# A new issue order for the first batch of a bucketed attention with a gated projection, with unread matmuls and another PSUM home for scale scratch

## The chip, the core and the metric

The kernel runs on one core of a Trainium2 chip. The metric is the device time of one execution in microseconds (us). The engines are TensorE (PE in the profile), VectorE (DVE), ScalarE (ACT), GpSimd (POOL) and SyncE (SP), which here issues every DMA. Each engine works through its own instructions in the order in which they were issued to it. Where an instruction needs something of another engine or of a DMA, it waits on a semaphore, and everything behind it on its engine waits with it.

## The reference

Four batches of eight heads, 768 tokens and head size 64. Keys and queries get six sign bits from a projection; a query sees only keys with the same six bits. The attention output feeds two projections whose product is projected again.

```python
B, H, S, D = 4, 8, 768, 64
q_bucket = sum(((q @ proj) > 0) * 2 ** arange(6));  k_bucket = ...     # proj is 64 x 6
mask = q_bucket[:, :, :, None] == k_bucket[:, :, None, :]
scores = where(mask, (q @ k.T) / 8, -1e9)
attn = exp(scores - max(scores));  attn = attn / (sum(attn) + 1e-9)
x = (attn @ v).transpose(0, 2, 1, 3).reshape(3072, 512)
out = ((x @ w_a) * (x @ w_b)) @ w_out                                  # w_a, w_b: 512 x 1536
```

## The kernel before

Every float32 operand of a matmul is split into two 16-bit parts (a high one and the rest), scaled by powers of two, so one product takes two or three matmuls in 16 bits.

**Preparation.** Keys of two heads at a time (`kprep`), queries of all heads for a third of the sequence, called a chunk (`qprep`), and values (`vprep`) are loaded, their largest magnitude is found (L785, L782, L998), spread over all partitions by a small matmul against an identity (`spread`, L450), turned into a power of two (`scale_of`, L456 to L478), and the data are split (L922 ACT, L934 or L938 copy, L943 DVE). A transposition by DMA (L883) brings each half to the layout that PE wants; for the first key pair and the first query chunk PE transposes instead (L894, `turn`). Bucket bits come from a matmul of 12 columns (L855, `buckets`) and are written as marks (L868) beside the data, so that a score of unequal buckets comes out hugely negative. The weights are prepared in the same manner (`words`, `to_f32`, `w_scale`, `hi_lo`: L563 loads, L659 largest magnitude, L592, L599 and L606 joining, L678 or L679 and L683 splitting).

**Attention.** A unit is a batch, a chunk and half of the heads, written 0_0_1 for batch 0, chunk 0, half 1; it has eight tiles (`qtile`) of 128 queries by 768 keys, written 0_0_1_j_h_t. A tile goes scores on PE (L1065), largest on DVE (L1077), width and bias (L1086, L1093 or L1099), exponential on ACT (L1109), cast to 16 bits (L1117 to L1119), subtraction of the cast (L1129 on POOL or L1133 on DVE), DMA transposition (L1139), and attention times values on PE (L1148). Scores have two PSUM buffers (tag `s`). When a unit's tiles are done, `su_end` scales the result, and after the second half it makes `xT` for the chunk.

**Projections.** `moe` takes the 1536 inner columns in twelve blocks of 128. A block is 24 matmuls into a PSUM buffer `ab` (L1351), ACT (L1365), DVE (L1373), a cast (L1381 or L1385), POOL (L1393), then six matmuls into `o` (L1403). `ab` and `o` have one PSUM buffer each. Block 0_2_3 is batch 0, chunk 2, block 3.

**The order.** The functions only record operations. `ORDER` (L96 to L290) is a list of operation numbers in the order of issue; a number plus 10000 or 20000 picks another engine for an operation that has such a choice, and a negative number -n would call `fill(n)` (L1513), which issues n matmuls into a buffer called `warm` that nobody reads. The list before has no negative number. Each engine's order of work is the order of its operations in the list. A tile of PSUM or SBUF with one buffer is handed on in the same order, so a matmul into `o` waits until whoever had `o` before has been read.

Of the kernel before, what the change touches and what calls it, by code (L numbers as in the profile page):

```python
# [45 lines left out]
SUMS = [1, 0]  # L46
# [15 lines left out]
QK = float(2.0**14)  # L62
LEAST = 16.0
# [6 lines left out]
def constants():  # L70
# [219 lines left out]
]  # L290


# [1263 lines left out]
```

## Time and profile before

| what | us |
|---|---|
| median of 3 runs (lowest, highest) | 929.32 (927.99, 933.16) |
| the profiled execution, its own time | 935.07 |
| its span, first to last instruction | 933.0 |
| PE busy in the span | 848.7 |
| DVE, ACT, POOL busy in the span | 665.3, 542.3, 445.2 |

The profiled execution took 2.07 us more than its span, and 5.75 us more than the median of the runs. The page divides the span into 40 slices of 23 us. In its row for PE the first ten slices are below the rest, which stand at 9 (90% or more) nearly to the end; the row for DVE is high over the first twelve slices or so; and the row PEclk, the clock that was granted to PE in tenths of full speed, dips in slices 3 to 5.

### The profile page before, as it was taken

To read this page: it belongs to the slowest core of one execution; us is meant where nothing else is said; L and a number is where in the kernel's file an instruction comes from. 1 tells how busy PE (TensorE), PEld (TensorE's weight loads), DVE (VectorE), ACT (ScalarE), POOL (GpSimd) and SP (SyncE) were. 2 spreads that over 40 slices of the span, in tenths; PEclk is the share of its full clock that TensorE was granted. 3 is DMA by queue.
4 is the path that set the end of the run, shared out by engine and by line. 5 is a ranking of instruction groups with operands and counts; after the bars stand their busy time and mean duration, and the time that the engine had idled before them with its cause. 6 is when DMAs were issued, how large, how long until landed. Compare 5 with 4: busy or idle time off the path is not lost.

```text
span 933.0 us, 22762 instructions
## 1 busy us (share of the span) xinstructions
PE 848.7 (91%) x9042; PEld 632.3 (68%) x9042; DVE 665.3 (71%) x1576; ACT 542.3 (58%) x1039; POOL 445.2 (48%) x384
## 2 busy tenths in 40 slices
PE   2656696989999999999999999999999999999998
PEld 2334464666777777777777777777777777777775
DVE  7888889879887868877866756876877964752311
ACT  5887889778853566554545446553566646453222
POOL 1556857666753445453253264554444745352111
PEclk9956799899999999999999999999999999999999
DMA  8999999999598769989857657888968974744000
GB/s 321 215 236 227 219 214 235 234 195 232 132 183 176 133 133 203 194 170 198 161 90 139 129 124 173 155 160 178 188 157 166 165 124 93 142 109 69 1 24 22
DMA packets 445353, 149.69 MB, mean 160 GB/s; under 512 B 416960, under 2 KB 437568, under 8 KB 445248
## 3 DMA queue, kind: packets, MB, share of 16 engines
q1 hardware_dynamic: 445248, 148.25, 77.7%
q8 instruction: 70, 1.15, 0.5%
q14 instruction: 35, 0.29, 0.1%
HBM read 37.85 MB, written 6.29 MB: 47 GB/s over the span
## 4 chain that ended last, share of the span: by engine, by line
PE 50%; DVE 17%; DMA 8%; issue 5%; ACT 5%; POOL 3%; SPq 1%; ACTq 0%; DVEq 0%; POOLq 0%
PE ab L1351 25%; PE o L1403 12%; PE s L1065 7%; PE av L1148 5%; DVE mx L1077 4%; DMA at<-a 4%; ACT e L1109 2%; DMA vr<-in_v_dram 2%; DVE g L1373 2%; POOL a L1129 2%; DVE a L1133 1%; ACT a L1118 1%; DMA rk_k<-in_k_dram 1%; DVE xz L1248 1%; DVE nB_k L943 1%
## 5 line engine op out<-in xcount | busy, mean ns | idle before, releaser
L1351 PE MATMUL ab<-xT,wab 128*128 128x256 f16 x3456 | 407.4, 273 | 7.8 <-DVE g L1373 7.3
L1351 PEld LDWEIGHTS <-wab 128*128 128x128 f16 x3456 | 333.9, 98 | 62.1 <-issue 11.4
L1129 POOL TENSOR_TENSOR a<-e,a 128x768 f16<-128x768 f32 x145 | 242.5, 1676 | 122.7 <-ACT a L1118 61.3
L1109 ACT ACTIVATE e<-s,bias,width 128x768 f32<-128x768 f32 x192 | 189.7, 989 | 88.6 <-DVE bias L1099 74.1
L1393 POOL TENSOR_TENSOR g<-g,g 128x256 f16<-128x256 f32 x144 | 106.5, 739 | 245.8 <-ACT g L1381 152.8
L1077 DVE TENSOR_REDUCE mx<-s 128x1 f32<-128x768 f32 x192 | 181.4, 950 | 45.5 <-PE s L1065 45.0
L1403 PE MATMUL o<-wo,g 128*128 128x512 f16 x864 | 210.4, 381 | 0.0
L1148 PEld LDWEIGHTS <-at 128*128 128x128 f16 x3456 | 128.7, 101 | 45.1 <-DMA at<-a 24.4
L1148 PE MATMUL av<-vh,at 128*128 128x64 f16 x2304 | 131.3, 197 | 20.0 <-DMA at<-a 18.9
L1373 DVE SCALAR_TENSOR_TENSOR g<-ab,wlow,a 128x256 f32<-128x256 f32 x120 | 57.7, 481 | 109.9 <-ACT a L1365 101.7
L1403 PEld LDWEIGHTS <-g 128*128 128x128 f16 x864 | 82.1, 98 | 75.2 <-issue 1.4
L1365 ACT ACTIVATE a<-ab,wlow 128x256 f32<-128x256 f32 x120 | 56.4, 470 | 123.1 <-PE ab L1351 117.2
L1065 PE MATMUL s<-kTA_k,qTA_q 128*128 128x384 f16 x384 | 101.0, 347 | 23.7 <-ACT e L1109 15.1
L1065 PE MATMUL s<-kTB_k,qTB_q 128*128 128x384 f16 x384 | 101.4, 348 | 0.0
L1118 ACT CAST a<-e 128x768 f16<-128x768 f32 x97 | 80.0, 828 | 6.5 <-DMA at<-a 5.1
L1119 POOL CAST a<-e 128x768 f16<-128x768 f32 x55 | 47.3, 860 | 71.5 <-ACT e L1109 67.0
L1093 ACT ACTIVATE bias<-mx,width 128x1 f32<-128x1 f32 x92 | 26.2, 291 | 74.5 <-DVE width L1086 74.2
L1381 ACT CAST g<-g 128x256 f16<-128x256 f32 x102 | 41.0, 402 | 46.5 <-DVE g L1373 38.4
L1148 PE MATMUL av<-vl,at 128*128 128x64 f16 x1152 | 67.9, 197 | 0.0
L1065 PEld LDWEIGHTS <-qTA_q 128*128 128x128 f16 x384 | 35.3, 101 | 47.7 <-issue 23.0
L1065 PEld LDWEIGHTS <-qTB_q 128*128 128x128 f16 x384 | 39.8, 104 | 29.5 <-issue 7.4
L1133 DVE TENSOR_TENSOR a<-e,a 128x768 f16<-128x768 f32 x47 | 50.3, 1073 | 3.5 <-ACT a L1118 3.2
(199 smaller groups left out, 757.6 us busy)
## 6 DMA issues: line engine op xcount, KB each, us to landing
rk_k<-in_k_dram SPq DMA_DIRECT2D x16, 384.0 KB, 4.1
vr<-in_v_dram SPq DMA_DIRECT2D x16, 384.0 KB, 4.3
rq_q<-in_q_dram SPq DMA_DIRECT2D x12, 512.0 KB, 5.1
out_dram<-ob SPq DMA_DIRECT2D x24, 256.0 KB, 2.4
raw_wo<-in_moe_w_out_dram SPq DMA_DIRECT2D x8, 512.0 KB, 5.4
at<-a SPq DMA_TRANSPOSE x192, 3.7
raw_w0ab<-in_moe_w_a_dram SPq DMA_DIRECT2D x4, 512.0 KB, 9.1
wab<-in_moe_w_b_dram SPq DMA_DIRECT2D x4, 512.0 KB, 8.0
```

The source lines that it names most:

```text
L1065: nc.tensor.matmul(ps.t[:, jj, :HALF], lhsT=x.t[:, uq, :], rhs=y.t[:, h * NT + jj * 3 : h * NT + jj * 3 + 3, :].rearrange("p t x -> p (t x)"),
L1077: lambda: nc.vector.tensor_reduce(out=mx.t[:, u : u + 1], in_=halves(ps.t), axis=AX.XY, op=ALU.max, negate=True),
L1109: lambda: nc.scalar.activation(flat2(e.t), halves(ps.t), AF.Exp, bias=bias.t[:, u : u + 1], scale=width.t[:, u : u + 1], accum_out=sm.t[:, ...
L1118: ("ACT", 0.725, lambda: nc.scalar.copy(out=a2.t[:, 0], in_=e.t), False),
L1129: lambda: nc.gpsimd.tensor_tensor(out=a2.t[:, 1], in0=e.t, in1=a2.t[:, 0], op=ALU.subtract),
L1133: lambda: nc.vector.tensor_tensor(out=a2.t[:, 1], in0=e.t, in1=a2.t[:, 0], op=ALU.subtract), True,
L1148: nc.tensor.matmul(av.t[:, u, :], lhsT=at.t[:, a + kt, :], rhs=w.t[:, h, kt, :], start=i == 0, stop=i == 3 * NT - 1,)
L1351: nc.tensor.matmul(pl.t[:, m, :CH], lhsT=wt(m, wi, cc, f), rhs=xt.t[:, :, xi * NC + cc, :], start=i == 0, stop=i == 3 * NC - 1,)
L1365: lambda a=a, pl=pl, gr=gr: nc.scalar.activation(a.t, pl.t[:, 0, :CH], AF.Copy, scale=cuts[:, gr : gr + 1]),
L1373: lambda a=a, g32=g32, pl=pl, gr=gr: nc.vector.scalar_tensor_tensor(out=g32.t, in0=pl.t[:, 1, :CH], scalar=cuts[:, gr + 1 : gr + 2], in1=a ...
L1393: lambda g=g, g32=g32: nc.gpsimd.tensor_tensor(out=g[1].t, in0=g32.t, in1=g[0].t, op=ALU.subtract),
L1403: nc.tensor.matmul(po.t[:, u, :], lhsT=g[gi].t[:, us], rhs=wo[f // 2].t[:, f % 2, wi * DM : (wi + 1) * DM], start=f % per_q == 0 and i == ...
```

## The change

Three edits.

1. `ORDER` is new for about the first 1250 of its 3638 operations; behind that the same operations stand in nearly the same order. The list names the same operations; for some three per cent of them it picks another engine.
2. The list now has 37 negative numbers, from -1 to -17, that sum to 246: `fill` issues 246 matmuls of 128 columns of weights against 256 moving columns in 16 bits. Nothing reads their result. All stand ahead of the first matmul of the projections; the last stands just before the scores of tile 0_1_1_1_0_1. `fill` takes the PSUM buffer `ab`.
3. Six small matmuls that spread a largest magnitude (projection, first-batch keys, first weights) used `ab` as scratch; they now use `o`, which the bucket and PE-transposition results of the first batch use too.

```diff
@@ ORDER, two lines of the new list
+    17, 261, 78, 18, 20, 64, 80, 19, 21, 82, 10022, 65, -6, 83, 66, 84, 10028, 68, 89, -14, 29, 30, 85, 296, -3, 23,
+    42, 97, 92, 98, -11, 36, 103, 37, 306, 20099, 112, 104, 38, 100, 10052, 43, 113, 44, -7, 53, 105, 114, 101,
...
@@ proj_parts
-        scale_of(mx, sc.t, pinv, ["pinv", sc], "proj", -85, tag="ab")
+        scale_of(mx, sc.t, pinv, ["pinv", sc], "proj", -85, tag="o")
@@ w_groups
-            [(x, 2 * fq + m) for x in ("wcut", "wone") for m in ms], name, key + 4, "s" if fq else "ab",
+            [(x, 2 * fq + m) for x in ("wcut", "wone") for m in ms], name, key + 4, "s" if fq else "o",
@@ kprep
-            SUMS[0], (B, "hi"), tag=tag if b else "ab", least=LEAST, top=QK,
+            SUMS[0], (B, "hi"), tag=tag if b else "o", least=LEAST, top=QK,
```

`fill` itself stood in the kernel before, uncalled:

```python
def fill(n):
    if not warm:
        warm.append(pp.tile([P, 2, CH], F32, tag="ab", name="warm", bufs=1))
    for _ in range(n):
        nc.tensor.matmul(
            warm[0][:, 0, :], lhsT=ident16, rhs=ident16.unsqueeze(1).to_broadcast([P, 2, P]), start=True, stop=True
        )
```

Three places show what moved. Names are cut by the listing: the batch number is left out (all are batch 0), so `s_0_1_0_1_1` is the scores of tile 0_0_1_0_1_1, and a last number of several digits is a buffer's serial number. The changed file is one line longer, so its line numbers are one higher.

The first place is PE at the first two tiles of scores. Before, the two follow each other, behind the scale of the third key pair.

```order
L450 LDWEIGHTS mx_k_2_351
L450 MATMUL ps_k_2_358<-identb,mx_k_2_351 128x128
L1065 LDWEIGHTS qTA_q_0_356
L1065 MATMUL s_0_0_0_0_0_372<-kTA_k_0_292,qTA_q_0_356 128x384
...
L1065 MATMUL s_0_0_0_0_1_380<-kTA_k_0_292,qTA_q_0_356 128x384
...
L855 LDWEIGHTS kTB_k_1_329
L855 MATMUL b_k_1_385<-pjk,kTB_k_1_329 128x12
```

Now seven unread matmuls stand ahead of the first tile (one of them is shown), and the scale, eleven more and a bucket matmul stand between the two tiles.

```order
L1518 LDWEIGHTS ident_65
L1518 MATMUL warm<-ident_65 128x256
L1066 LDWEIGHTS qTA_q_0_392
L1066 MATMUL s_0_0_0_0_0_419<-kTA_k_0_326,qTA_q_0_392 128x384
...
L451 MATMUL ps_k_2_427<-identb,mx_k_2_361 128x128
L1518 LDWEIGHTS ident_65
...
L856 MATMUL b_k_1_457<-pjk,kTB_k_1_395 128x12
...
L1066 MATMUL s_0_0_0_0_1_470<-kTA_k_0_326,qTA_q_0_392 128x384
```

The scale of key pair 2 and the bits of pair 1 both take `o` now, one after the other, and unread matmuls stand in front of each tile.

The second place is SP's queue from the transposition of tile 0_0_0_0_1_0 on. Before, weight loads (L563) stand among the transpositions of attention (L1139) and of preparation (L883).

```order
L1139 DMA_TRANSPOSE at_0_0_0_1_0_478<-a_0_0_0_0_1_0_458 128x12x128
L563 DMA wab<-in_moe_w_out_dram 128x1024
L1139 DMA_TRANSPOSE at_0_0_0_1_1_557<-a_0_0_0_0_1_1_464 128x12x128
L883 DMA_TRANSPOSE kTA_k_2_559<-marked 128x12x128
L1139 DMA_TRANSPOSE at_0_0_1_0_0_588<-a_0_0_0_1_0_0_542 128x12x128
L883 DMA_TRANSPOSE qTB_q_1_621<-nB_q_1_439 128x16x128
L1139 DMA_TRANSPOSE at_0_0_1_0_1_629<-a_0_0_0_1_0_1_583 128x12x128
L563 DMA raw_w1ab_0_675<-in_moe_w_b_dram 128x1024
L1139 DMA_TRANSPOSE at_0_0_1_1_0_677<-a_0_0_0_1_1_0_623 128x12x128
L883 DMA_TRANSPOSE qTA_q_1_710<-marked 128x16x128
L883 DMA_TRANSPOSE kTB_k_3_743<-nB_k_3_579 128x12x128
L563 DMA raw_w1ab_0_675<-in_moe_w_b_dram 128x1024
```

Now no load stands there.

```order
L1140 DMA_TRANSPOSE at_0_0_0_1_0_610<-a_0_0_0_0_1_0_558 128x12x128
L884 DMA_TRANSPOSE kTA_k_2_632<-marked 128x12x128
L1140 DMA_TRANSPOSE at_0_0_0_1_1_661<-a_0_0_0_0_1_1_607 128x12x128
L884 DMA_TRANSPOSE kTB_k_3_718<-nB_k_3_490 128x12x128
L1140 DMA_TRANSPOSE at_0_0_1_0_0_729<-a_0_0_0_1_0_0_617 128x12x128
L1140 DMA_TRANSPOSE at_0_0_1_0_1_776<-a_0_0_0_1_0_1_663 128x12x128
L1140 DMA_TRANSPOSE at_0_0_1_1_0_803<-a_0_0_0_1_1_0_731 128x12x128
L884 DMA_TRANSPOSE kTA_k_3_813<-marked 128x12x128
L1140 DMA_TRANSPOSE at_0_0_1_1_1_863<-a_0_0_0_1_1_1_778 128x12x128
L1140 DMA_TRANSPOSE at_0_1_0_0_0_915<-a_0_0_1_0_0_0_830 128x12x128
L884 DMA_TRANSPOSE qTB_q_1_925<-nB_q_1_695 128x16x128
L1140 DMA_TRANSPOSE at_0_1_0_0_1_966<-a_0_0_1_0_0_1_892 128x12x128
```

Weight loads have moved to before this stretch or behind it, the key transpositions have moved forward and the second query chunk's back.

The third place is DVE between the fourth and fifth tile of unit 0_0_1. Before, the first use of a loaded piece of `w1ab` (L659) and three joins of weights (L606) stand between them.

```order
L1077 TENSOR_REDUCE mx_0_1_680<-s_0_1_0_1_1_769 128x1
L864 TENSOR_REDUCE b_k_3_783<-b_k_3_783 128x72
L868 TENSOR_SCALAR marked<-b_k_3_783 128x12x6 x2
L1086 TENSOR_SCALAR width_0_1_700<-mx_0_1_680,qsig_q_0_296 128x1
L659 TENSOR_REDUCE wmx_w1ab<-raw_w1ab_0_675 128x1
L1099 TENSOR_SCALAR bias_0_1_702<-mx_0_1_680,width_0_1_700 128x1
L606 SCALAR_TENSOR_TENSOR wab<-wab 128x1024
L606 SCALAR_TENSOR_TENSOR wab<-raw_w0ab_1_149 128x1024
L606 SCALAR_TENSOR_TENSOR wo_y_872<-wab 128x1024
L1187 TENSOR_TENSOR x_0_0_877<-av_0_0_482,r_0_0_740 128x512
L1077 TENSOR_REDUCE mx_0_1_680<-s_0_1_1_0_0_883 128x1
```

Now only the small operations of the fourth tile stand there.

```order
L1078 TENSOR_REDUCE mx_0_1_768<-s_0_1_0_1_0_832 128x1
L1087 TENSOR_SCALAR width_0_1_781<-mx_0_1_768,qsig_q_0_323 128x1
L1100 TENSOR_SCALAR bias_0_1_796<-mx_0_1_768,width_0_1_781 128x1
L944 SCALAR_TENSOR_TENSOR nB_q_1_695<-rq_q_1_90,qsc_q_1_726,nB_q_1_695 128x16x64
L1078 TENSOR_REDUCE mx_0_1_768<-s_0_1_0_1_1_868 128x1
L1087 TENSOR_SCALAR width_0_1_781<-mx_0_1_768,qsig_q_0_323 128x1
L1100 TENSOR_SCALAR bias_0_1_796<-mx_0_1_768,width_0_1_781 128x1
L1078 TENSOR_REDUCE mx_0_1_768<-s_0_1_1_0_0_935 128x1
```

The joins, the largest magnitude of `w1ab` and the scaling of the unit 0_0_0 have moved behind the fifth tile.

## Rows read from the trace of the kernel before

**Rows 1.** Busy us by engine in five stretches, with granted PE clock and DMA share.

```profile
core 0: us, PE busy (x) PEld busy (x) DVE busy (x) ACT busy (x) POOL busy (x), PEclk, DMA share, GB/s
0.00:40.00 40.00, 16.75 (x127) 11.01 (x128) 30.72 (x78) 28.44 (x38) 10.69 (x14) 1.00 0.89 273
40.00:120.00 80.00, 50.75 (x551) 33.85 (x550) 66.09 (x153) 65.08 (x102) 55.23 (x37) 0.66 1.08 227
120.00:240.00 120.00, 102.08 (x1162) 74.39 (x1161) 108.58 (x238) 98.72 (x174) 75.44 (x55) 0.96 1.08 223
240.00:300.00 60.00, 59.03 (x610) 44.74 (x609) 48.32 (x126) 34.83 (x66) 34.25 (x29) 1.00 0.75 154
300.00:920.00 620.00, 611.66 (x6545) 462.95 (x6543) 410.11 (x982) 311.81 (x653) 267.53 (x248) 1.00 0.70 136
```

**Rows 2.** Chain of waits, 0 to 300 us: start, us, what.

```profile
115.38 1.28 PE s L1065 x4
...
267.12 1.31 PE ab L1351 x12
268.43 0.65 PE s L1065 x4
```

**Rows 3.** PE's timeline near 29 us: start, us, instruction, idle before.

```profile
28.63 0.82 PE L1065 MATMUL s<-kTA_k,qTA_q 128*128 128x384 f16 x2 [1.85 <-ACT qTA_q L902]
29.25 0.85 PE L1065 MATMUL s<-kTB_k,qTB_q 128*128 128x384 f16 x2
29.89 0.85 PE L1065 MATMUL s<-kTA_k,qTA_q 128*128 128x384 f16 x2
```

**Rows 4.** Who DVE waited for, 0 to 120 us: total, times, longest.

```profile
DVE mx L1077 <- PE s L1065: 7.6, 11, 2.2
DVE wmx_w1ab L659 <- DMA raw_w1ab<-in_moe_w_b_dram: 3.0, 2, 1.6
DVE mx_k L785 <- DMA rk_k<-in_k_dram: 3.0, 1, 3.0
DVE mx_v L785 <- DMA vr<-in_v_dram: 1.7, 1, 1.7
DVE wmx_w1ab L659 <- DMA wab<-in_moe_w_a_dram: 1.4, 1, 1.4
```

**Rows 5.** Who PE waited for, 0 to 120 us.

```profile
PE s L1065 <- ACT e L1109: 11.9, 12, 3.0
PE av L1148 <- DMA at<-a: 10.2, 6, 3.4
...
PE b_k L855 <- DVE pjk L523: 2.8, 1, 2.8
```

**Rows 6.** DVE's timeline between two tiles of unit 0_0_1.

```profile
68.71 0.69 DVE L659 TENSOR_REDUCE wmx_w1ab<-raw_w1ab 128x1 f32<-128x512 f32 x1 [1.35 <-DMA raw_w1ab<-in_moe_w_b_dram]
...
71.70 2.67 DVE L606 SCALAR_TENSOR_TENSOR wo_y<-wab 128x1024 int32<-128x1024 int32 x1
```

**Rows 7.** SP's timeline from 44 us.

```profile
44.96 1.40 SPq L1139 DMA_TRANSPOSE at<-a  x1
46.46 3.35 SPq L883 DMA_TRANSPOSE kTA_k<-marked  x1
49.92 1.43 SPq L1139 DMA_TRANSPOSE at<-a  x1
```

**Rows 8.** Groups of DVE, 0 to 300 us: busy us, mean ns | idle before.

```profile
L1133 DVE TENSOR_TENSOR a<-e,a 128x768 f16<-128x768 f32 x9 | 11.9, 1322 | 0.4 <-ACT a L1118 0.3
L943 DVE SCALAR_TENSOR_TENSOR nB_q<-rq_q,qsc_q,nB_q 128x1024 f16<-128x1024 f32 x5 | 7.4, 1490 | 0.1
...
L1117 DVE CAST a<-e 128x768 f16<-128x768 f32 x3 | 2.9, 951 | 0.2
L785 DVE TENSOR_REDUCE mx_k<-rk_k 128x1 f32<-128x768 f32 x3 | 2.8, 947 | 3.0 <-DMA rk_k<-in_k_dram 3.0
...
L938 DVE COPY marked<-nB_k 128x768 f16<-128x768 f16 x2 | 1.8, 909 | 0.3 <-DMA qTA_q<-marked 0.3
...
L679 DVE CAST wab<-wab 128x1024 f16<-128x1024 f32 x2 | 1.4, 686 | 0.0
...
L1004 DVE TENSOR_REDUCE qmx_q<-rq_q 128x1 f32<-128x1024 f32 x1 | 1.2, 1211 | 0.0
```

**Rows 9.** Groups of ACT, 0 to 300 us.

```profile
L1118 ACT CAST a<-e 128x768 f16<-128x768 f32 x45 | 37.0, 826 | 5.6 <-DMA at<-a 5.1 <-ACT e L1109 0.3
L678 ACT CAST wab<-wab 128x1024 f16<-128x1024 f32 x9 | 9.4, 1043 | 4.4 <-DVE wab L606 4.4
```

**Rows 10.** PE's small scale matmuls, 0 to 120 us.

```profile
L450 PE MATMUL ps_k<-identb,mx_k 128*128 128x128 bf16 x4 | 1.2, 295 | 10.5 <-ACT nB_k L782 5.6 <-DVE mx_k L785 4.9
```

**Rows 11.** SP's timeline from the start.

```profile
0.74 0.47 SPq L769 DMA_DIRECT2D rk_k<-in_k_dram  x1
...
2.85 0.58 SPq L769 DMA_DIRECT2D vr<-in_v_dram  x1
```

385 rows, old and new, of the table ORDER are left out of this document.

## The prediction

> **What bounds the kernel now.** I read the stretches first [rows 1]. From 300 to 920 us PE is busy 611.66 of 620 us at a granted clock of 1.00: there the end is set by PE alone, and other engines have room (DVE 410 us busy, ACT 312). From 240 to 300 it is the same, 59.03 of 60. Ahead of that PE is not full: it stands idle 23.3 us of the first 40, 29.3 of the next 80 and 17.9 of the next 120, 70.4 us in all. Much of what it does there is slow, too. From 40 to 120 us the granted clock is 0.66. In the first 40 us the column shows 1.00, but the matmuls do not: four scores matmuls start 0.64 us behind the last four [rows 3], where a tile takes 0.65 us at full speed and 1.28 us in a slow stretch [rows 2]. So PE ran at its lower level, 1.2 GHz, there too. Half of 16.75 us and 0.34 of 50.75 us are 8.4 + 17.3 = 25.6 us of PE time lost to the clock in the first 120 us, and 0.04 of 102.08, 4.1 us, in the next 120.
>
> What keeps PE from filling up in the first 240 us is the work that feeds it: DVE is busy 96.8 of the first 120 us and 108.6 of the next, ACT 93.5 and 98.7, the DMA share is 0.89 and then 1.08 [rows 1]. No single one is full; they wait for each other. So the change is worth what it takes from PE's unused time before about 300 us, and nothing behind that point can give or take much.
>
> **The change part by part.** *What is ahead of the point where PE is full.* I take block 0_2_3 of the projections, near 300 us, and count by the two orders what stands ahead of it on each engine. On PE it is the same matmuls, plus the 246 unread ones. On ACT three more casts of exponentials (0.826), two more weight casts (1.043) and some smaller ones that nearly cancel: +3.2 us [rows 9]. On DVE three subtractions (1.322), two casts (0.951), two largest magnitudes of keys (0.947) and two weight casts (0.686) fewer, 9.1 us; three more copies (0.909), a query split (1.490) and a query's largest magnitude (1.211), and four subtractions of weights, which the rows show on no DVE: between the 1.2 us that would be 0.909 x 1024 / 768 and the 1.8 us that is 1.322 x 1024 / 768 I take 1.5; with small ones (1.9) that makes 13.3 us [rows 8]. So DVE has some 4 us more (3 to 5.5), ACT 3, POOL less. In the first 300 us DVE idles 46.3 us and ACT 73.0 [rows 1], so most of it finds room: I put it at +1.0 us, between 0 and 4.
>
> *The unread matmuls.* Twelve matmuls of the same shape take 1.31 us [rows 2], 0.109 each, so 246 take 26.9 us at full clock and about twice that, 53, at the lower one. They stand ahead of all projections, that is inside the first 120 us or so, where PE idles 52.5 us [rows 1]. I cost them at nothing, covered by that idle time; without cover they cost up to 26.9. What they may give back is clock. PE's scores come late for DVE 11 times in the first 120 us, 7.6 us in all [rows 4]; a tile's scores at full clock take half as long (0.65 for 1.28 us), so I take half of it, 3.8 us, between 0 and 7.6. What PE waits for itself, 11.9 us for exponentials and 10.2 for transpositions [rows 5], a faster PE does not shorten.
>
> In this trace the clock falls again and again, so that 25.6 us of PE's first 120 were lost to it, 2.7% of the span [rows 1]. The Trainium skill (TensorE: Matmul & The Clock Gate, What's actually happening) says that the throttled state is the default and that activity releases it, and advises for modeling that "the ramp penalty is <1% of a typical kernel span". By that sentence clock edits here could give at most 9.3 us; by the row 25.6 us of PE time are slow, of which the 3.8 us are all that I see on a path.
>
> *SP and the loads.* Between 44 and 51 us SP issues one transposition after the other, and single issues last 1.40, 3.35 and 1.43 us with nothing between them [rows 7]: its queue is full there, and a load in it delays the transpositions behind it. The new order has no load in that stretch. On DVE the three joins and the wait of 1.35 us for a piece of `w1ab` that stand between two tiles of unit 0_0_1, 68.71 to 74.4 us [rows 6], move behind the tiles. DVE waits for loads 3.0 + 3.0 + 1.7 + 1.4 = 9.1 us in the first 120 [rows 4]. The two on `w1ab`, 4.4 us, should go, since the uses move back; those on the first keys and values stay. I take 4.5 us, between 0 and 9.1.
>
> *The start.* The first keys are now the fifth DMA, not the first: the fifth issue begins 2.1 us behind the first [rows 11]. Against it the projection is loaded first, and PE waits 2.8 us for it now [rows 5]. I take 0, between +2.1 and -0.7.
>
> *Scratch in `o`.* Six scale matmuls now share one buffer with bits and transposition results. Each holds it for its matmul, 0.295 us [rows 10], and a reduction about as long, so 0.6; if every one held up what follows, 3.6 us. All but the first stand in a stretch in which PE waits anyway: 0.
>
> Sum: 1.0 - 3.8 - 4.5 = -7.3 us. The profiled execution had a span of 933.0 and took 935.07; it would be 925.7 and 927.8. The runs' median is 929.32, 5.75 below the profiled one, and I take the change off that: 922.0 us.
>
> **The rivals.** *The waits change places.* The waits for scores and loads go, but the tiles go through the same two score buffers, and transpositions over a DMA that is over its full share from 40 us on (1.08). Then 9.1 + 7.6 us of waits come back as waits for exponentials and transpositions, PE's 22.1 us of them [rows 5] grow, and only the added DVE work or nothing is left: 929 to 930 us. For it: DVE 81% and ACT 78% busy in the first 120 us, so little room. Against it: three joins and a wait in front of a tile are gone in plain sight.
>
> *The larger gain.* Nearly all waits of DVE for scores and loads go (16.7 us), and some of PE's idle 17.9 us between 120 and 240 as well, as projections start on a fuller queue: 929.3 - 18 = 911 us. Against it: those waits are what a full set of engines leaves at the best of times.
>
> *Slower: unread matmuls in the way.* PE takes its work in order. A run of n unread matmuls that comes up when the next scores are ready holds them by n x 0.109 us (0.21 at the lower clock), a mean of 6.6, that is 0.7 to 1.4 us, 37 times. The gaps for them were laid out ahead, and issues on SP last 1.40 to 3.35 us [rows 7], so the real gaps will lie elsewhere. It decides once more than 7.3 of the 26.9 us are on the path, some 27%. At half of them, 13.5 us, it is 929.3 - 7.3 + 13.5 = 935.5 us. Against it: PE idles twice as long as they take. For it: at the lower clock they take as long as all of PE's idle time, 53 against 52.5 us, and then every mismatch is on the path.
>
> *The clock does not stay up.* The unread matmuls may be too thin to hold it. Then 3.8 us go from the sum: 925.8 us, inside the likeliest case's own range.
>
> **How the numbers follow.** The forecast with its own range of 917 to 927 has 0.40, the exchange of waits 0.26, the larger gain 0.18, the slower case 0.16. Within 0.5% is 924.7 to 934.0 us; that is about what measurement can tell from no change. Of the forecast 0.32 lies below 924.7 and 0.08 above; with the larger gain and 0.03 of the exchange that makes 0.53 faster; 0.08 + 0.23 = 0.31 the same; 0.16 slower. The bounds of the terms added up on one side are 929.3 - 7.6 - 9.1 - 0.7 = 912, and 908 with part of the idle time behind 120 us; on the other, 936 with half of the unread matmuls on the path. The range is 908 to 936.
>
> **What would show it.** In the changed profile the clock from 40 to 120 us should be above 0.9, and scores near 29 us should take 0.65 us a tile. DVE's waits for scores in the first 120 us should be at 4 us or below, and none for `w1ab` should stand in unit 0_0_1. Tile 0_0_1_1_1_1 should come earlier than now, by about the 5.7 us that the joins and their wait take, and PE's real work (without the unread matmuls) up to 300 us should be 7 us more. It is wrong if the clock holds and block 0_2_3 is no earlier: then the bound ahead of it is DVE, ACT and the DMAs together, and waits have only moved. It is wrong the other way if scores are held by unread matmuls, which would show as PE busy on `warm` while DVE waits for scores.

## The result, and the profile after

| kernel | median us (lowest to highest, runs) | ratio to before, 95% interval |
|---|---|---|
| changed | 937.66 (932.93 to 940.52, 10) | 1.0053 [1.0027, 1.0079] |
| before, on the same chip | 933.0 (927.99 to 936.22, 10) | 1 |

The change made the kernel slower by half a per cent; 922.0 us and a gain of 0.8% had been forecast, from a median of 929.32 us of three runs of the kernel before; its ten runs here have 933.0. The profiled execution of the changed kernel took 934.51 us, 3.1 below its median, and that of before 935.07, 2.1 above its own. So the two traces, with spans of 932.7 and 933.0 us, show the same length. What follows is read for where time moved inside; how much the whole moved is told by the runs' medians.

The five stretches of the changed kernel, the columns as in [rows 1]:

```profile
core 0: us, PE busy (x) PEld busy (x) DVE busy (x) ACT busy (x) POOL busy (x), PEclk, DMA share, GB/s
0.00:40.00 40.00, 23.92 (x217) 17.55 (x218) 31.78 (x85) 29.07 (x39) 10.52 (x15) 0.97 0.92 299
40.00:120.00 80.00, 60.91 (x765) 44.61 (x764) 66.08 (x148) 66.59 (x114) 57.22 (x36) 0.91 1.12 235
120.00:240.00 120.00, 100.29 (x1127) 73.63 (x1124) 104.17 (x232) 97.30 (x159) 76.25 (x54) 0.97 0.98 199
240.00:300.00 60.00, 55.71 (x587) 41.79 (x586) 51.95 (x133) 37.32 (x75) 28.59 (x26) 1.00 0.89 168
300.00:920.00 620.00, 611.70 (x6550) 463.41 (x6549) 423.60 (x980) 316.95 (x655) 266.38 (x248) 1.00 0.69 136
```

PE's clock from 40 to 120 us rose from 0.66 to 0.91. Behind 300 us PE is as busy as before (611.70 us after 611.66). But from 120 to 300 us PE, DVE and the DMA share are not what they were: the DMA share of 120 to 240 us fell from 1.08 to 0.98 and that of 240 to 300 rose from 0.75 to 0.89. Over 0 to 300 us the shares times the lengths make 296.6 us before and 297.4 now: about the same transfers, in part later.

The waits of DVE in the first 120 us, to be set against [rows 4]:

```profile
DVE mx L1078 <- PE s L1066: 8.2, 7, 2.4
DVE pmx L511 <- DMA pj<-in_proj_dram: 4.2, 1, 4.2
DVE x L1188 <- PE av L1149: 2.4, 1, 2.4
```

No wait for a load of keys, values or `w1ab` is left of the 9.1 us; a wait for the projection (4.2) and one for a product (2.4) are new, and the waits for scores are 8.2 us after 7.6. So little was gained in all: DVE is idle 120 - 31.78 - 66.08 = 22.1 us of the first 120, after 23.2 [rows 1]. The waits for scores are not a matter of PE's speed, for near 27 us scores run at full clock where they had not [rows 3]; PE's timeline, with an unread portion between two tiles:

```profile
26.60 0.50 PE L1066 MATMUL s<-kTA_k,qTA_q 128*128 128x384 f16 x2 [0.52 <-ACT qTA_q L903]
26.94 0.49 PE L1066 MATMUL s<-kTB_k,qTB_q 128*128 128x384 f16 x2
27.26 0.22 PE L451 MATMUL ps_k<-identb,mx_k 128*128 128x128 bf16 x1
27.32 1.36 PE L1518 MATMUL warm<-ident 128*128 128x256 f16 x11
```

The tile takes 27.26 - 26.60 = 0.66 us. PE itself waits less in the first 120 us, where unread matmuls now fill some of its time, but for the same two things (11.9 and 10.2 us before, [rows 5]):

```profile
PE s L1066 <- ACT e L1110: 8.9, 12, 1.8
PE av L1149 <- DMA at<-a: 8.6, 7, 2.3
```

SP's queue after 45 us, to be set against [rows 7], has hardly a gap there either:

```profile
45.33 1.27 SPq L1140 DMA_TRANSPOSE at<-a  x1
46.70 1.52 SPq L884 DMA_TRANSPOSE kTB_k<-nB_k  x1
48.38 3.48 SPq L1140 DMA_TRANSPOSE at<-a  x2
```

Where the lead went is seen by counting, with the program's order laid beside the trace. The exponential of tile 0_0_1_1_1_1 starts at 75.7 us after 84.1, that of tile 0_1_1_1_0_0 at 112.9 after 127.0. But block 0_2_3 starts at 298.3 after 297.9. Two counts tell it. The first is PE's time that no read matmul has used: the time less the read matmuls begun by then, each at its mean distance from start to start behind 300 us (scores 0.162 us, `ab` 0.109, `av` 0.029, `o` 0.216, and the small ones of the preparation likewise). The second is how many transpositions and other DMAs SP has begun.

| by us | 120 | 140 | 200 | 240 | 300 |
|---|---|---|---|---|---|
| PE's unused time, before | 79.7 | 82.7 | 100.0 | 105.8 | 107.5 |
| changed | 76.3 | 83.8 | 97.2 | 102.5 | 107.9 |
| changed, second profile (e5) | 77.0 | 83.8 | 98.0 | 104.1 | 109.9 |
| transpositions / others begun, before | 34 / 36 | | 63 / 49 | 75 / 58 | 89 / 66 |
| changed | 36 / 37 | | 61 / 50 | 69 / 58 | 89 / 66 |

Fourteen us of lead in attention are worth 3.4 us of PE's time at 120 us, since PE is little used there. At 140 and at 300 us nothing is left of the lead; that it is there again at 200 is 2 to 3 us, no more than single profiles of one order differ (the kernel of e2 below, in the old order, is 3.3 us from the kernel before at 200). SP's queue has the same 89 transpositions and 66 others behind it at 300 us in both kernels: it got two ahead by 120 us and six behind by 240.

### The profile page after: what moved, and what is told of

The parts are those of the page before. It is cut to its first block, busy times and chain, and to the rows that moved or that the text cites. A ratio compares the mean times of both kernels' runs of the same rounds, so it can differ in the third digit from the quotient of the medians.

```text
span 932.7 us, 23260 instructions
## 1 busy us (share of the span) xinstructions
PE 860.7 (92%) x9288; PEld 646.2 (69%) x9288; DVE 678.7 (73%) x1576; ACT 550.7 (59%) x1046; POOL 441.0 (47%) x379
## 5 line engine op out<-in xcount | busy, mean ns | idle before, releaser
L1130 POOL TENSOR_TENSOR a<-e,a 128x768 f16<-128x768 f32 x148 | 249.1, 1688 | 141.5 <-ACT a L1119 76.5
L1394 POOL TENSOR_TENSOR g<-g,g 128x256 f16<-128x256 f32 x144 | 103.3, 717 | 248.3 <-ACT g L1382 152.0
L1149 PEld LDWEIGHTS <-at 128*128 128x128 f16 x3456 | 124.9, 99 | 41.5 <-DMA at<-a 23.1
L1149 PE MATMUL av<-vh,at 128*128 128x64 f16 x2304 | 128.8, 195 | 18.7 <-DMA at<-a 18.6
L1066 PE MATMUL s<-kTA_k,qTA_q 128*128 128x384 f16 x384 | 95.9, 332 | 17.5 <-ACT e L1110 12.8
L1066 PE MATMUL s<-kTB_k,qTB_q 128*128 128x384 f16 x384 | 95.9, 332 | 0.0
L1119 ACT CAST a<-e 128x768 f16<-128x768 f32 x100 | 82.5, 828 | 10.7 <-DMA at<-a 8.3
L1134 DVE TENSOR_TENSOR a<-e,a 128x768 f16<-128x768 f32 x44 | 42.5, 969 | 9.6 <-ACT a L1119 9.4
```

The costliest lines, as they stand in the source:

```text
L1066: nc.tensor.matmul(ps.t[:, jj, :HALF], lhsT=x.t[:, uq, :], rhs=y.t[:, h * NT + jj * 3 : h * NT + jj * 3 + 3, :].rearrange("p t x -> p (t x)"),
L1119: ("ACT", 0.725, lambda: nc.scalar.copy(out=a2.t[:, 0], in_=e.t), False),
L1130: lambda: nc.gpsimd.tensor_tensor(out=a2.t[:, 1], in0=e.t, in1=a2.t[:, 0], op=ALU.subtract),
L1149: nc.tensor.matmul(av.t[:, u, :], lhsT=at.t[:, a + kt, :], rhs=w.t[:, h, kt, :], start=i == 0, stop=i == 3 * NT - 1,)
L1394: lambda g=g, g32=g32: nc.gpsimd.tensor_tensor(out=g[1].t, in0=g32.t, in1=g[0].t, op=ALU.subtract),
```

## Experiments

Theory 1: the lead is given back, since DVE and ACT have the same work ahead of block 0_2_3. Theory 2: unread matmuls hold scores. Theory 3: the choice of engines costs. Theory 4: the scratch costs. Theory 5: the order behind 120 us alone is slower. Theories 6 and 7 came with the later runs: the DMA side sets the pace, by all that it carries (6) or by transpositions alone (7). Each ratio is to the kernel before, run beside it; the changed kernel's median in what follows is 937.6 us (e5).

**The parts of the change.** e1 takes the 37 portions out of the list:

```diff
-    17, 261, 78, 18, 20, 64, 80, 19, 21, 82, 10022, 65, -6, 83, 66, 84, 10028, 68, 89, -14, 29, 30, 85, 296, -3, 23,
+    17, 261, 78, 18, 20, 64, 80, 19, 21, 82, 10022, 65, -1, 83, 66, 84, 10028, 68, 89, 29, 30, 85, 296, 23,
```

> The changed kernel with its order and its scratch in the output's buffer, without the unread matmuls (one of the 246 is left, near the start, since it opens the buffer of the projections). Theory 1, the lead is given back: up to block 0_2_3 DVE, ACT and the DMAs together set the pace, PE has room whatever its clock, so PE's clock falls again between 40 and 120 us (below 0.8 against 0.91 in the changed kernel) and the time is that of the changed kernel within 0.3%: ratio to the kernel before 1.003 to 1.008. Theory 2, unread matmuls stand in the way of needed scores: without them the loss goes, ratio 0.998 or below, and DVE's waits for scores in the first 120 us fall from 8.2 us to under 5. A third way, the unread matmuls are what the new order lives on: ratio over 1.010.

Measured: 935.53 us, 1.0042 [1.0024, 1.0059]. So the unread matmuls neither hold scores nor carry the order; theory 2 falls. The clock stayed higher than every theory had it, 0.85 from 40 to 120 us with one unread matmul in place of 246:

```profile
40.00:120.00 80.00, 49.52 (x605) 33.93 (x604) 67.34 (x151) 68.82 (x116) 59.83 (x38) 0.85 1.13 238
```

e2 is the old list with the three `tag="ab"` of the diff as `tag="o"`, and a -1 near the start.

> The kernel before with the scale scratch in the output's buffer as the only change (and one unread matmul near the start, which opens the buffer of the projections). Theories 1 and 2: no change, ratio 0.998 to 1.002. Theory 4, the shared buffer makes six scale matmuls and the transpositions' results follow one another: up to 3.6 us and what follows on it, ratio 1.003 to 1.005.

Measured: 932.4 us, 1.0004 [0.9984, 1.0023]. The scratch costs nothing; theory 4 falls.

e3 is that list with the 37 portions of the new one, each ahead of the same PE operation (two of them, 22 matmuls, some operations earlier).

> The kernel before in its old order, with the same 246 unread matmuls in the same 37 portions, each ahead of the operation of TensorE that it precedes in the changed kernel (two portions, 22 in all, come some operations earlier, since the projections use their buffer by then), and the scratch in the output's buffer. Theory 1: the clock of 40 to 120 us rises from 0.66 to over 0.85 and the time stays: ratio 0.997 to 1.003, since PE does not set the pace there. Theory 2: here the portions meet gaps that were not planned for them, so they hold scores more than in the changed kernel: ratio 1.005 to 1.015. If the clock is what was wanted in the old order: ratio below 0.996.

Measured: 930.69 us, 0.9987 [0.9967, 1.0006]. The clock of the stretch is 0.89, and the time is that of before within 0.4%:

```profile
40.00:120.00 80.00, 59.68 (x774) 45.81 (x772) 67.63 (x162) 67.26 (x109) 56.14 (x36) 0.89 1.11 233
```

e4 keeps the new order and gives each operation the engine of the old list (a number's 10000 or 20000 taken from there).

> The changed kernel with its order, its unread matmuls and its scratch, but each operation of the list on the engine that the old list chose for it (112 operations of the whole list differ; ahead of block 0_2_3 it takes about 4 us of work from DVE and 3 from ACT and gives 7 to POOL). Theory 3, the choice of engines eats the lead: block 0_2_3 comes 4 us or more earlier than in the changed kernel (298 us), ratio to the kernel before 1.000 or below. Theory 1, the order itself piles the deferred work up ahead of 283 to 298 us: ratio 1.003 to 1.010, and block 0_2_3 within 2 us of 298.

Measured: 943.14 us, 1.012 [1.009, 1.015], block 0_2_3 at 306.2 us. The new choice of engines is better for the new order, not worse; theory 3 falls. With scratch, unread matmuls and engines each tried, what is left as slower is the order itself.

**Which part of the order.** e5 is the changed kernel again.

> The changed kernel once more, for a second profile and for runs on the chip of the next three. Every theory: ratio 1.003 to 1.008. By the traces so far the time from the first matmul of block 0_2_3 to the end is the same in all kernels (631.0 to 632.5 us), so whatever its time is, block 0_2_3 should stand at the end's time less 632 us, within 1.5 us.

Measured: 937.6 us, 1.0064 [1.0045, 1.0083]. Block 0_2_3 starts at 300.4 us and the engines' last instruction ends at 932.6, so 632.2 us, as expected; to the end of the span, 935.5, it is 635.1, and 933.0 - 297.9 = 635.1 in the kernel before. What comes behind this block hardly changes (632.5 to 637.4 us to the end of the span over all profiles), and nearly all of the difference between the kernels arises ahead of it.

e6 joins the first 500 operations of the new list, with the unread matmuls, with what is left of the old; e7 joins the first 450 of the old with what is left of the new, with one unread matmul alone.

> The first 500 operations in the new order (up to the first block of projections, near 117 us) with all unread matmuls, what is then left in the old order, each operation on the engine of the list that places it. Theory 1, the lead of the first 120 us is paid back by whatever order follows, since the work put off comes due: ratio 1.001 to 1.007. Theory 5, the loss lies in the order of the rest alone (transpositions that hold scores at 120 to 160 us, DVE's full stretch at 240 to 280): ratio 0.988 to 0.998, block 0_2_3 before 295 us.

> The first 450 operations in the old order (up to the first block of projections, near 119 us), what is then left in the new order. Theory 1: the new rest has less left to pay back here, ratio 0.997 to 1.004. Theory 5, the new rest itself is the slower: ratio 1.006 to 1.015, and TensorE loses 5 us or more between 240 and 280 us, as in the changed kernel (there 5.4 us of its time have no read matmul, 1.7 in the kernel before).

Measured: e6 959.64 us, 1.0298 [1.0276, 1.032]; e7 947.81, 1.0173 [1.015, 1.0196]. Both joined lists are worse than either whole, beyond what any theory gave. It may be that an order cut in two has its own price where the halves meet; at any rate the halves can't be priced this way, and these two runs settle nothing on theory 5.

e8 gives 14 operations between block 0_1_7 and block 0_2_3 to the engine that the number without its 10000 names (POOL or ACT for DVE); three of them:

```diff
-10417 ... 10422 ... 10756
+417 ... 422 ... 756
```

> The changed kernel with 14 operations that stand between block 0_1_7 and block 0_2_3 (228 to 298 us) taken from DVE: by their durations DVE has 8.4 us less there, POOL 10.3 and ACT 3.6 more. Theory 1 in its narrow form, DVE's full stretch of 240 to 280 us is where the lead is lost: TensorE's loss there falls from 5.4 us to under 3, ratio 0.999 to 1.003. Theory 5 in its narrow form, the loss there comes from transpositions and loads that come late (or from the earlier stretch): ratio 1.004 to 1.008.

Measured: 935.66 us, 1.005 [1.0032, 1.0069]. DVE was relieved (45.36 us busy from 240 to 300 us, 51.95 in the changed kernel), the time was not. The narrow form of theory 1 falls.

**Which engine sets the pace.** e9 to e12 do one thing twice for 12 of batch 0's 48 tiles. For the exponentials:

```diff
+        again = 2 if b == 0 and h and t else 1
-            lambda: nc.scalar.activation(flat2(e.t), halves(ps.t), AF.Exp, ...),
+            lambda: [nc.scalar.activation(flat2(e.t), halves(ps.t), AF.Exp, ...) for _ in range(again)],
```

> The changed kernel, in which DVE computes the row maxima of 12 of batch 0's 48 score tiles twice (every fourth tile, between 30 and 200 us): 12 x 0.950 = 11.4 us more work on DVE and nothing else. Theory 1, DVE and ACT together set the pace ahead of block 0_2_3: of the 11.4 us 6 to 11 reach the end, the median goes from 937.6 to 943.5 or later. Theory 6, transpositions on the DMA queue set it: under 4 us, below 941.5.

> The changed kernel, in which ACT computes the exponentials of the same 12 tiles twice: 12 x 0.99 = 11.9 us more on ACT. Theory 1: 4 to 11 us reach the end, 941.5 or later. Theory 6: under 4 us, below 941.5.

> The changed kernel, in which POOL computes the low parts of the same 12 tiles twice: 12 x 1.69 = 20.3 us more on POOL. Theory 1: POOL has room (77 us idle in 80 to 240 us and before), under 5 us reach the end, below 942.5. Theory 6: the low part is what a transposition waits for (44.5 us of the SP queue's waits in the first 300 us end with it), so 10 us or more reach the end, 947 or later.

> The changed kernel, in which the transpositions of the same 12 tiles are issued twice: 12 more, each 1.4 to 3.3 us of the SP queue, so 17 to 40 us more there. Theory 1: under 8 us reach the end, below 945.5. Theory 6: 10 us or more, 947.5 or later.

| twice | more work, us (12 times its mean) | median us | against 937.6 | ratio to before |
|---|---|---|---|---|
| e9, DVE maxima | 11.4 | 939.83 | +2.2 | 1.0086 [1.0069, 1.0104] |
| e10, ACT exponentials | 11.9 | 936.58 | -1.0 | 1.0053 [1.0034, 1.0073] |
| e11, POOL low parts | 20.3 | 936.57 | -1.0 | 1.0063 [1.004, 1.0086] |
| e12, transpositions | 12 of them | 979.21 | +41.6 | 1.0504 [1.0477, 1.0531] |

Theory 1 falls: of DVE's work a fifth reaches the end, and by the intervals perhaps none; of ACT's and POOL's nothing that can be told from none. DVE is 8 us busier from 40 to 120 us, and in the first 120 it waits for scores 3.4 us where it waited 8.2; the trace of e9, its row of the stretch and then its wait for scores:

```profile
40.00:120.00 80.00, 56.09 (x752) 41.09 (x752) 74.09 (x156) 66.76 (x113) 56.93 (x37) 0.98 1.11 234
```

```profile
DVE mx L1080 <- PE s L1067: 3.4, 4, 2.0
```

In e12 the cost is more than the issue of 12 transpositions. The waits of SP's queue in the first 300 us of e12 say why: the second transposition of a tile waits for the first to land.

```profile
SPq L1142 <- DMA at<-a: 32.7, 13, 4.7
```

The added issues last 1.27 us or more each as well, some 17 us in all by the timeline. So about 50 us of the queue's time, 32.7 of them standstill, cost 41.6 us at the end.

e13 asks whether loads in the same queue cost as much:

```diff
-                lambda i=i, raw=raw, at=at: nc.sync.dma_start(out=raw.t[...], in_=src[...]),
+                lambda i=i, raw=raw, at=at: [nc.sync.dma_start(out=raw.t[...], in_=src[...])
+                    for _ in range(2 if name.startswith("w1ab") else 1)],
```

> The changed kernel, in which the 8 loads of the second group of weights (512 KB each, issued between 67 and 107 us) are issued twice: 4 MB more over the DMA engines, and 0.3 to 0.6 us more of the SP queue for each. At 217 GB/s, the mean of the first 300 us, that is 19 us of the DMA engines' time; at 331 GB/s, the mean of the first 23 us, 12.7. Theory 6, sharpened: the DMA engines, full from 20 to 200 us, set the pace ahead of block 0_2_3, whatever they carry: 10 to 19 us reach the end, ratio 1.016 to 1.027. Theory 7, only transpositions cost, by their own queue and not by the engines' share: under 5 us, ratio under 1.011.

Measured: 965.52 us, 1.0359 [1.0338, 1.038], beyond both theories. Again the second waits for the first, 17.3 + 8.1 + 7.8 = 33.2 us of SP's waits in the first 300 us:

```profile
SPq L565 <- DMA raw_w1ab<-in_moe_w_b_dram: 17.3, 4, 4.7
...
SPq L565 <- DMA wab<-in_moe_w_a_dram: 8.1, 2, 4.7
SPq L565 <- DMA raw_w1ab<-in_moe_w_a_dram: 7.8, 2, 4.0
```

Beside these 33.2 us of standstill stand 27.9 at the end. And the DMA engines were not fuller for it, but emptier, 1.00 after 1.12:

```profile
40.00:120.00 80.00, 53.35 (x657) 39.41 (x654) 55.58 (x128) 56.36 (x96) 45.79 (x30) 0.85 1.00 212
```

So neither theory as put: it is not transpositions alone (7), and the engines' share is not shown to be the limit (6). What both runs show is that some 33 us of standstill in SP's queue, through which every load and transposition goes in order, reach the end for the most part, where 11 to 20 us of DVE's, ACT's or POOL's work reach it hardly or not. Both runs also move more bytes (12 x 384 KB and 8 x 512 KB), so the queue's time and the engines' are not taken apart.

**Taking work from that queue.** e14 to e18 transpose some tiles of batch 0 on PE, which has time there, into the PSUM buffer `o`. Until the first output (at 145.3 us in the changed kernel) only scratch and small results of the preparation use it:

```diff
+        def by_pe():
+            got.append(pp.tile([P, 2, 512], F32, tag="o", name=f"tt_{n}", bufs=1))
+            out = got[0].rearrange("p a b -> p (a b)").bitcast(F16)
+            ...
+            for i in range(2 * NT):
+                nc.tensor.transpose(out=out[:, i * P : (i + 1) * P], in_=src[:, i * P : (i + 1) * P], identity=ident16)
+        def to_sbuf():
+            nc.scalar.copy(out=at.t..., in_=got[0]...)          # e18: nc.vector.tensor_copy
```

In the list the tile's DMA goes. For most tiles the transposition stands two PE operations ahead of the tile's products and the copy one.

> The changed kernel, in which 6 of batch 0's 48 tiles are transposed on TensorE (12 blocks each into the output's PSUM, then one copy by ACT) and not by DMA. Theory 6: 6 x 3.5 us (what a transposition more cost) = 21 us less DMA time; ACT takes on 6 copies of some 1.3 us, which cost nothing by the run with the exponentials doubled. Block 0_2_3 5 to 20 us earlier, ratio to the kernel before 0.985 to 1.000. Theory 1: DVE and ACT set the pace, so no gain: 1.004 to 1.015.

> The same with 13 of the 48 tiles. Theory 6: up to 45 us of DMA time less, ACT 17 us more; below the run with 6 tiles, ratio 0.970 to 0.992, until DVE and ACT (81% and 83% busy from 40 to 120 us) set the pace. Theory 1: 1.005 to 1.025, above the run with 6.

> The old order with the 246 unread matmuls in their portions (ratio 0.9987 by itself) and 13 of the 48 tiles transposed on TensorE. Theory 6: the same relief of the DMA engines as in the run before, ratio 0.970 to 0.992; the order of the list counts for less than the relief, so within 1% of the run with 13 tiles in the new order. Theory 1: 1.000 to 1.020.

> The old order with the 246 unread matmuls in their portions and 7 of batch 0's 48 tiles transposed on TensorE, copied by ACT. Theory 6, the DMA engines set the pace: 7 x 3.5 = 24 us less DMA time, the new order with 6 tiles gained 9 us; so 5 to 12 us below the old order with unread matmuls (930.7), ratio 0.985 to 0.994. If the copies that ACT takes on cost as much as the DMA time is worth in the old order (13 tiles there lost 10 us): 0.996 to 1.005.

> The changed kernel with 6 of batch 0's 48 tiles transposed on TensorE, as in the run at 0.997, the copies by DVE and not by ACT. By the doubled work (DVE 2.2 of 11.4 us reached the end, ACT none of 11.9) 6 copies on DVE cost 1 us more at the end: ratio 0.996 to 1.000. If ACT's place in the order is what the copies disturb: under 0.994.

| kernel | median us | ratio to before | block 0_2_3 at, us (one profile) |
|---|---|---|---|
| e14, new order, 6 tiles, ACT copies | 928.46 | 0.997 [0.9953, 0.9988] | 295.2 |
| e18, new order, 6 tiles, DVE copies | 928.85 | 0.9968 [0.9947, 0.9988] | 288.8 |
| e15, new order, 13 tiles, ACT copies | 943.31 | 1.0114 [1.009, 1.0138] | 309.0 |
| e17, old order with unread matmuls, 7 tiles | 938.97 | 1.0071 [1.0047, 1.0095] | 301.2 |
| e16, the same, 13 tiles | 940.65 | 1.0095 [1.0076, 1.0114] | 305.5 |

Six transpositions less on SP's queue give the changed kernel 9.1 and 8.8 us back, and both versions beat both kernels, the one before by 0.3%. By 240 us PE's unused time in e18 is 94.0 us, after 102.5 and 104.1; its profiled execution took 923.89 us, 5.0 below its median, and that of e14 931.36, 2.9 above, so that their blocks 0_2_3 stand 6.4 us apart at equal medians. The groups of e18 show what the six tiles cost the engines, 5.0 us on PE and 5.7 on DVE:

```profile
L1154 DVE COPY at<-tt 128x1536 f16<-128x1536 f16 x6 | 5.7, 953 | 0.9 <-PE tt L1151 0.9
L1151 PE MATMUL tt<-ident,a 128*128 128x128 f16 x72 | 5.0, 219 | 1.6 <-DVE xT L1321 1.6
```

With 13 tiles the gain turns into a loss, and in the old order 7 lose too, against what I expected of both. The list was made for transpositions by DMA; a PE transposition stands in PE's queue and waits there for its input, and the copy waits for it on its own engine. In e17 ACT waits 3.9 us for the transpositions, in e14 1.0:

```profile
L1154 ACT COPY at<-tt 128x1536 f16<-128x1536 f16 x7 | 10.1, 1436 | 5.1 <-PE tt L1151 3.9 <-PE av L1171 1.2
```

Against e3 (930.69) the loss is 8.3 us with 7 tiles and 10.0 with 13, and these waits are 5.1 us, so why the old order does not profit is not settled. Nor is the loss of e15, where ACT waits 1.1 us for them: its transpositions run until 150.7 us, and the first `ab` and the first output come 12 and 14 us later than in the changed kernel, at 129.4 and 159.1, but no run takes one PSUM buffer and PE's order apart.

The Trainium skill (VectorE: DVE Perf Modes, Rules for kernel authors) advises TensorE for a 128 x 128 transposition where PSUM may be its target, and DMA otherwise. Six tiles in the new order agree; 13 tiles, and 7 in the old order, do not. The Trainium skill also says (Advanced Engine Details and Errata, X-Bar Transpose (TRN2)) that DMA transpositions are as fast as other DMAs. The trace agrees: 3.7 us from issue to landing for a tile's 384 KB, 3.9 and 4.3 for loads of that size, medians of the changed kernel's whole execution.

```profile
vr<-in_v_dram SPq DMA_DIRECT2D x16, 384.0 KB, 3.9
rk_k<-in_k_dram SPq DMA_DIRECT2D x16, 384.0 KB, 4.3
...
at<-a SPq DMA_TRANSPOSE x192, 3.7
```

## Why the prediction was wrong

**The step that failed** is the pair of terms -3.8 and -4.5: half of DVE's stalls for scores and loads taken out, and taken as time at the end. The stalls did not go, they changed places. The waits for keys, values and `w1ab` went, all of the 9.1 us; but 4.2 us for the load of the projection and 2.4 for a product came, and those for scores stayed, 8.2 after 7.6. DVE's idle time in the first 120 us fell by 1.1 us, from 23.2 to 22.1, where 8.3 were forecast. The clock held, and still block 0_2_3 came no earlier, at 298.3 and 300.4 us after 297.9. This is the sign that the prediction gave for itself being wrong, "if the clock holds and block 0_2_3 is no earlier: then the bound ahead of it is DVE, ACT and the DMAs together, and waits have only moved". The runs correct that, too: it is not DVE and ACT. DVE's time is worth a fifth at the end at most (2.2 of 11.4 us) and ACT's nothing, while e12 and e13, with 32.7 and 33.2 us of standstill in SP's queue, end 41.6 and 27.9 us later. I had read this queue as full, "its queue is full there, and a load in it delays the transpositions behind it", and drew from it that loads should leave the stretch. But the same loads came through the same queue later, with all 89 transpositions and 66 other DMAs still ahead of 300 us. A load put off comes back to the same queue ahead of the same block; no run moves the loads alone.

**The clock.** Right that it holds (0.91, above 0.9) and that a tile's scores there take 0.65 us (0.66 near 27 us). The working has a slip that changes nothing: in [rows 3] it is two matmuls, not four, that start 0.64 us behind the last two, so a tile takes 1.26 us, the lower level. Wrong that the clock is worth 3.8 us: DVE waits 8.2 us for scores, not 4 or less, and in the old order the raised clock is worth 1.7 us (932.4 to 930.69) with overlapping intervals. The Trainium skill (TensorE: Matmul & The Clock Gate, What's actually happening) puts the ramp penalty below 1% of a typical kernel span, here 9.3 us as an estimate from that figure, and these runs agree. Of the 25.6 us of PE time that the low clock had cost, no more than these 1.7 us can have been on the path in that order.

**More work on DVE and ACT, +1.0.** The size is not contradicted: at a fifth, 4 us on DVE are 0.8 us. One reading behind it is loose: the two groups named for ACT make 4.6 us, and the small ones that bring it to 3.2 do not nearly cancel.

**The unread matmuls, 0, and the scratch, 0.** Both right. e1 is 2.1 us below the changed kernel and e3 1.7 below e2, and both pairs of intervals overlap. The rival that had unread matmuls in the way of scores did not happen; that its time, 935.5 us, is near the result is chance.

**The start, 0.** DVE now waits 4.2 us for the projection, and the first exponential still starts at 29.8 us after 31.7. No run tests it alone.

**The marks.** No `w1ab` wait in unit 0_0_1, as forecast; tile 0_0_1_1_1_1 8.4 us earlier, not 5.7; PE's read work up to 300 us 0.4 us less, not 7 more.

**The rival that came nearest** in kind is that of waits that change places, at 929 to 930 us. It is what DVE's waits did, and it named the full DMA share as its reason. It had no term for a loss of the order itself: 4.0 us by e1 (935.53 less 931.58) and 6.1 by e5 (937.6 less 931.52). What the traces show of that loss is the stretch of 120 to 240 us, in which SP begins 33 transpositions in the changed kernel and 41 before. Its issues there last 85.9 us after 97.9: the queue is not fuller, it stands still 12 us longer. The two longest of the changed kernel stand before a key's transposition that waits for DVE's marks and before a tile of batch 1 that waits for its low part; SP's timeline around the one and the other:

```profile
185.31 0.88 SPq L770 DMA_DIRECT2D rk_k<-in_k_dram  x1
192.98 1.43 SPq L884 DMA_TRANSPOSE kTA_k<-marked  x1
...
228.73 0.37 SPq L770 DMA_DIRECT2D rk_k<-in_k_dram  x1
244.33 3.00 SPq L1140 DMA_TRANSPOSE at<-a  x2
```

They last 6.8 and 15.2 us (10.9 of them ahead of 240 us), and 7.7 and 15.2 in the second profile; the longest of the kernel before from 120 to 300 us lasts 8.2 us. So at these places the queue waits for the engines. The view of waits names more, POOL's low parts from 120 to 200 us, first in the changed kernel and then in the one before:

```profile
SPq L1140 <- POOL a L1130: 18.4, 10, 3.6
```

```profile
SPq L1139 <- POOL a L1129: 4.7, 3, 3.5
```

But the view takes POOL's last signal before the end of an issue, whichever tile it is for. With each issue matched to its tile by the list, all 18 tiles of that stretch in the changed kernel had their low part done before the issue ahead had ended. So this is no wait of theirs, and 20.3 us more work on POOL cost nothing (e11). What the two standstills cost at the end was not tried, and whether the place of the transpositions in SP's queue is the cause stays open, as does the price of the order behind 120 us (e6 and e7).

## What to carry to other kernels

Before waits are added up, double the work of one engine at a time and see what reaches the end. Here 11 to 20 us more on DVE, ACT or POOL cost 2 us or nothing, though DVE and ACT were some 80% busy, while some 33 us of standstill in the in-order DMA queue cost 28 to 42. Look at an engine's whole idle time and not at the waits that a change removes: 9.1 us of them went here and the idle time fell by 1.1. A load that is only put off still has to pass the same queue ahead of the same point. Taking six of 48 transpositions out of that queue gave the changed kernel 9 us, more than the whole new order had been forecast to give; but 13 lost, and in the old order 7 lost too, so the order has to fit. A low clock of an engine that waits for others cost next to nothing here.

## What had not been expected of the hardware

- The clock from 40 to 120 us was 0.85 with one unread matmul in the new order (e1) and 0.66 to 0.69 in the old one (before, e2), with about the same PE busy time (49.52, 50.75 and 47.86 us, for 605, 551 and 542 matmuls): the order of the real work raises it, too.
- In e12 and e13 a second DMA to the same tile waits until the first has landed, and everything behind it in SP's queue waits too: 32.7 / 13 = 2.5 us (transpositions) and 33.2 / 8 = 4.2 us (512 KB loads) a time.
- Over all 20 profiled executions block 0_2_3 starts between 288.8 and 345.3 us, and from there to the end of the span it takes 632.5 to 637.4 us. The two profiles of the changed kernel differ by 2.8 us in span (932.7 and 935.5), 2.1 of it ahead of that block. Whether most of the 7 to 9 us by which runs of one kernel differ arises there too is not shown by two profiles.
